# Fused attention and expert routing: 608 slots per expert in place of 640, last tiles of 96 rows, eight result buffers in place of seven

## The chip, the cores and the metric

One core of a Trainium2 chip runs the whole program. The metric is the device time of one execution in microseconds; the runs before are summed up by the median of three. A profiled execution also gives a trace, whose span runs from the first to the last instruction of the core.

## What is computed

A pooled attention feeds a layer of eight experts, each a small two-layer network; every token goes to the one expert that its domain names. Cut to what matters:

```python
# attention: B, H, S, D = 8, 8, 1152, 64; neighbouring queries are averaged in pairs (576 left)
q_pool = q.reshape(B, H, S // 2, 2, D).mean(axis=3)
attn = softmax(q_pool @ k.T / sqrt(D))
x = (attn @ v).transpose(0, 2, 1, 3).reshape(4608, 512)     # one row per token
# experts: w1 is (8, 512, 1024), w2 is (8, 1024, 512)
for e in range(8):
    mask = domain_id == e
    out[mask] = np.maximum(x[mask] @ w1[e], 0.0) @ w2[e]
```

The domains are drawn at random but alike each time. Counted from the drawn input, the experts get 568, 557, 585, 576, 590, 599, 553 and 580 of the 4,608 tokens.

## The kernel before

The program has two stages that overlap. The attention stage computes the tokens' rows batch by batch and writes them in 16-bit form to a table in device memory (x_tok). Vector operations meanwhile work out which token stands in which slot of which expert. Each expert has CAP slots (L48, 640), cut into NTC tiles of 128 (L49): five tiles. Two lists hold, per slot, the row to gather (`grow`) and the row of the output to write (`gid`); a slot that no token fills reads row 0 of x_tok and has an output row beyond the last, whose write is dropped.

The first tiles of the experts 0 to 4 are computed inside the attention stage by `add_tile` (L793), in holes of TensorE's order. What is left is the expert stage from L1049 on, a list of ten *runs* made by `plan_runs` (L926). In this text they are run 0 (three tiles of expert 5, 384 rows), run 1 (one tile, 128 rows), runs 2 to 7 (the last two tiles of an expert each, 256 rows) and runs 8 and 9 (experts 6 and 7 whole, 640 rows). A tile is fetched by `get_x` (L680): an indirect DMA, issued by GpSimd, that gathers 128 rows of x_tok into a buffer `xs`. It must be turned, so that the 512 features lie on the partitions. For runs 2 to 7 TensorE does that (`turn_tile`, L1086, four matmuls against an identity into PSUM, then a copy by VectorE or ScalarE into `xt`); for runs 8 and 9 a transposing DMA on SyncE's queue does it (`flip_x`, L690).

One run is `stage1` (L1065) and `stage2` (L1098). Stage 1 makes the hidden layer: for each of 8 blocks f of 128 hidden units, four matmuls with a block of `w1h` as the weights and the run's slots as the moving columns, in pieces of at most 512 columns; ScalarE (f even) and VectorE (f odd) apply the maximum with 0 and write `hT`. Three PSUM buffers `hp` are shared by this and by the turned tiles. Stage 2 works tile by tile: eight matmuls with a block of `hT` (128 hidden units by the tile's rows) as the weights and 512 columns of `w2h` moving, then a copy of the PSUM result into a buffer `osb2` of the pool `ob` (L1059, seven buffers; ScalarE for a run's last tile and every second one before, VectorE for the others), then an indirect DMA from GpSimd (`scatter`, L525) that writes the tile's rows to the output. The two tiles of the next run are turned between the tiles of stage 2: in a run of two tiles, the first is turned ahead of the first tile's eight matmuls and the second ahead of the second tile's. The last tile of run 9 is split in two halves of 256 columns (L1103 to L1114).

A buffer of `ob` is taken again by the tile seven later, and its copy waits until the scatter that read it has landed. Each engine works its instructions in the order of the program; GpSimd's holds the gathers, the scatters and the weight loads (L509 to L519), whose transfers share one queue, and each of its DMAs waits for the landing of the one eight before it. SyncE's holds the transposing DMAs of runs 8 and 9.

The names in the rows: PE hp L1072 is stage 1, PE op L1117 stage 2, L1108 its split last tile, L1090 a turned tile, L675 a gather, L528 a scatter, L1077 and L1079 the maximum on ScalarE and VectorE, L1123 and L1125 the copies of results, L691 a transposing DMA, L633 the attention's product with v.

Of the kernel before, what the change touches and what calls it, by code (L numbers as in the profile page):

```python
# [9 lines left out]
P = 128  # L10
# [9 lines left out]
def kernel(  # L20
# [10 lines left out]
    nc = tc.nc  # L31
    B, H, S, D = q.shape
    Sp = S // 2
    N, Dm = out.shape
# [10 lines left out]
    NT = B * NQ  # L45
    KO = [0, 128, 256, 384]
    IB = [2 * NQ, 4 * NQ, 6 * NQ]
    CAP = 640  # L48
    NTC = CAP // P  # L49
    W = 432  # L50
    SPP = NC * Sp // W
    DV = D + 2
# [35 lines left out]
    ident16 = perm.tile([P, P], F16, name="ident16")  # L88
# [92 lines left out]
    for i in range(NV):  # L181
# [4 lines left out]
        out=lst[:, :], in_=lst[:, :], compare_op=ALU.is_ge, fill=1.0, base=0,  # L186
# [207 lines left out]
    gid = perm.tile([P, NH], I32, name="gid")  # L394
    grow = perm.tile([P, NH], I32, name="grow")
# [107 lines left out]
    wts = {}  # L503
# [21 lines left out]
    def scatter(dst, src, ap, group, bound=None):  # L525
        nc.gpsimd.memset(gap[:, :], 0.0)
        kw = {} if bound is None else {"bounds_check": bound, "oob_is_err": False}
        ins = nc.gpsimd.indirect_dma_start(  # L528
            out=dst[:, :],
            out_offset=bass.IndirectOffsetOnAxis(ap=ap, axis=0),  # L530
            in_=src,
            in_offset=None,
            **kw,
        )
        tc.declare_no_dep(ins.ins, group=group, reason="rows are unique")
        tc.add_to_no_dep_group(group, ins.ins)
# [136 lines left out]
    def gather(dst, ap, nb=B):  # L673
        nc.gpsimd.memset(gap[:, :], 0.0)
        nc.gpsimd.indirect_dma_start(  # L675
            out=dst, out_offset=None, in_=x_dram[0 : 1 + nb * Sp, :],
            in_offset=bass.IndirectOffsetOnAxis(ap=ap, axis=0),
        )

    def get_x(pool, e, i):  # L680
        x_ = pool.tile([P, Dm], F16, name="xs")
        mark(x_[0:1, 0:1], True)
        nb = [ib // NQ for k_, ib in zip(KO[1:], IB) if (i + 1) * P <= k_] + [B]
        assert len(kept) >= nb[0] * NQ
        gather(x_[:, :], grow[:, e * NTC + i : e * NTC + i + 1], nb[0])
        xs[e, i] = x_

    xs = {}

    def flip_x(dst, e, i):  # L690
        nc.sync.dma_start_transpose(dst, xs[e, i][:, :])  # L691

    WSTEP = [[20 + 40 * e + 10 * j for j in range(4)] for e in range(4)]
    WSTEP.append([174 + 6 * j for j in range(4)])
# [63 lines left out]
    for j in range(NJ):  # L758
        nc.tensor.transpose(
            qt[:, j * QP : (j + 1) * QP], in_=qp[0:QP, j, :, :].rearrange("p h d -> p (h d)"),  # L760
            identity=ident16[0:QP, 0:QP],
# [160 lines left out]
    xt = {0: xf[:, :].rearrange("p (n c) -> p n c", n=ND)}  # L922
    first = [(FILL, i) for i in range(NA)]
# [14 lines left out]
    for p in range(NPAIR - 1):  # L938
        lo = W * (p * SPP + (7 if p < 2 else 3))
# [18 lines left out]
    for t in range(NST + 4):  # L958
# [24 lines left out]
        if t == NST + 1:  # L983
# [3 lines left out]
            e, i0, i1 = next(r for r in runs if (r[0], r[1]) not in xs)  # L987
            for i in range(i0, i1):
                get_x(fxs, e, i)
        if main and want and t >= want[0][2] and t >= last_get + 5 and not (t in later) and not mmq and not rq:  # L990
            e, i, _ = want[0]
# [5 lines left out]
        if first and t >= max(got.get(first[0], NST) + 8, FLIPS[first[0][1]]):  # L997
            e, i = first.pop(0)
# [57 lines left out]
    tb = ctx.enter_context(tc.tile_pool(name="tb", bufs=2, reuse_waits="tile"))  # L1056
    tx = ctx.enter_context(tc.tile_pool(name="tx", bufs=4, reuse_waits="tile"))
    xov = ctx.enter_context(tc.tile_pool(name="xov", bufs=1, reuse_waits="tile"))
    ob = ctx.enter_context(tc.tile_pool(name="ob", bufs=7, reuse_waits="tile"))  # L1059
    wlast.append(ctx.enter_context(tc.tile_pool(name="wnext", bufs=1, reuse_waits="tile")))  # L1060

    def new_xt():
# [2 lines left out]
    def stage1(w1h, xt, m, at=None):  # L1065
        hT = tb.tile([P, NF, CAP], F16, name="hT")
        for f in range(NF):
            hp_ = hps.tile([P, 1024], FP32, name="hp")
            for lo in range(0, m, 512):
                n = min(512, m - lo)  # L1070
                for cc in range(ND):
                    nc.tensor.matmul(  # L1072
                        hp_[:, lo : lo + n], lhsT=w1h[:, cc, f * P : (f + 1) * P],
                        rhs=xt[:, cc, lo : lo + n], start=cc == 0, stop=cc == ND - 1,
                    )
            if f % 2 == 0:
                nc.scalar.activation(hT[:, f, 0:m], hp_[:, 0:m], AF.Relu)  # L1077
            else:
                nc.vector.tensor_scalar(  # L1079
                    out=hT[:, f, 0:m], in0=hp_[:, 0:m], scalar1=0.0, scalar2=None, op0=ALU.max  # L1080
                )
            if at and f in at:
                at[f]()
        return hT

    def turn_tile(dst, x_, i):  # L1086
        ps = hps.tile([P, 1024], FP32, name="hp")
        pv = ps[:, 0 : Dm // 2].bitcast(F16).rearrange("p (c r) -> p c r", c=ND)
        for cc in range(ND):
            nc.tensor.transpose(  # L1090
                pv[:, cc, :], in_=x_[:, cc * P : (cc + 1) * P], identity=ident16[:, :]
            )
        if i % 2 == 0:
            nc.vector.tensor_copy(dst, pv)
        else:
            nc.scalar.copy(dst, pv)

    def stage2(w2h, hT, n, ids, between=(), split=False, first=0):  # L1098
        between = list(between)
        for i in range(n):  # L1100
            for _ in range(-(-len(between) // (n - i)) if i >= first else 0):
                between.pop(0)()
            if split and i == n - 1:  # L1103
                osb = ob.tile([P, Dm], FP32, name="osb2")
                for lo, copy in ((0, nc.vector.tensor_copy), (Dm // 2, nc.scalar.copy)):
                    op_ = ops.tile([P, Dm], FP32, name="op")
                    for f in range(NF):
                        nc.tensor.matmul(  # L1108
                            op_[:, 0 : Dm // 2], lhsT=hT[:, f, i * P : (i + 1) * P],
                            rhs=w2h[:, f, lo : lo + Dm // 2], start=f == 0, stop=f == NF - 1,  # L1110
                        )
                    copy(osb[:, lo : lo + Dm // 2], op_[:, 0 : Dm // 2])
                scatter(out, osb[:, :], ids(i), "oscat", N - 1)
                break  # L1114
            op_ = ops.tile([P, Dm], FP32, name="op")
            for f in range(NF):
                nc.tensor.matmul(  # L1117
                    op_[:, :], lhsT=hT[:, f, i * P : (i + 1) * P], rhs=w2h[:, f, :],
                    start=f == 0, stop=f == NF - 1,
                )  # L1120
            osb = ob.tile([P, Dm], FP32, name="osb2")
            if i % 2 == (n - 1) % 2:
                nc.scalar.copy(osb[:, :], op_[:, :])  # L1123
            else:
                nc.vector.tensor_copy(osb[:, :], op_[:, :])  # L1125
            scatter(out, osb[:, :], ids(i), "oscat", N - 1)

    NR = NPAIR * 2 * NQ

# [37 lines left out]
    for k_, r in enumerate(runs):  # L1167
        e, i0, i1 = r
        n = i1 - i0
        while todo and todo[0][0] <= k_ + 2:  # L1170
            fetch(k_ + 2)
        btw = []
        if k_ == len(runs) - 1:
            nc.gpsimd.drain()
        for kn in (k_ + 1, k_ + 2, k_ + 3):
            if kn >= len(runs) or kn in xt or kn > k_ + 1 and kn < FLIP:
                continue
            xt[kn] = new_xt()
            en, j0, j1 = runs[kn]
            for j in range(j0, j1):  # L1180
                dst = xt[kn][:, :, (j - j0) * P : (j - j0 + 1) * P]
                if kn >= FLIP:
                    flip_x(dst, en, j)
                    continue
                btw.append(lambda dst=dst, en=en, j=j: turn_tile(dst, xs[en, j], j))
        get = lambda: fetch(len(runs))
        part = lambda: wq.pop(0)() if wq else None
        at = {1: get, 4: get, 6: get} if n < NTC else {1: get, 3: get, 5: get}
        if k_ < 2:
            at = {**at, 2: part, 7: part}  # L1190
        elif k_ >= len(runs) - 6:
            at = {**at, 2: part}
        h = stage1(wts[e][0], xt[k_], n * P, at)
        stage2(
            wts[e][1], h, n, lambda i, c=e * NTC + i0: gid[:, c + i : c + i + 1], btw,
            k_ == len(runs) - 1, first=n - 1 if k_ == 0 else 0,
        )
        if k_ in (3, 4):
            check_sums(k_ - 3)
        if i1 == NTC and e == 0 and rest:  # L1200
            er = rest.pop(0)
            fns, wts[er] = load_w(er)
            wq.extend(fns)
# [100 lines left out]
    def one_tile(w, og, oi):  # L1304
        xo = xov.tile([P, Dm], F16, name="xo")
        gather(xo[:, :], og)
        xto = new_xt()
        nc.sync.dma_start_transpose(xto[:, :, 0:P], xo[:, :])
        h = stage1(w[0], xto, P)
        stage2(w[1], h, 1, lambda i: oi)  # L1310

    anyx = nc.values_load(ovi[0:1, E : E + 1], min_val=0, max_val=N + 1)
    with tc.If(anyx > 0):
        bad = nc.values_load(ovi[0:1, E + 1 : E + 2], min_val=0, max_val=1)
        with tc.If(bad > 0):
            again()
            for e in range(E):
                fns, w = load_w(e)
                for fn in fns:
                    fn()  # L1320
                for i in range(NTC):
                    c = e * NTC + i
# [3 lines left out]
        for b in range(B):  # L1326
            for i in range(NQ):
                n = 64 if i == 0 else P
# [4 lines left out]
        for e in range(E):  # L1333
            fns, w = load_w(e)
# [3 lines left out]
            with tc.For_i(0, nt, 1) as j:  # L1338
                oi = xov.tile([P, 1], I32, name="oi")
# [3 lines left out]
                    out=og[:, :], in0=oi[:, :], scalar1=1.0, scalar2=None, op0=ALU.add  # L1343
                )
                nc.vector.tensor_scalar(
                    out=og[:, :], in0=og[:, :], scalar1=float(N), scalar2=None, op0=ALU.min
# [30 lines left out]
```

## Time and profile before

| | us |
|---|---|
| device time, median of 3 runs (lowest to highest) | 417.11 (416.21 to 419.22) |
| device time of the profiled execution | 416.44 |
| its span, first to last instruction | 414.4 |

The device time of the profiled execution lies 2.0 us above its span, and 0.7 us below the median. Stage times below are read from the profiled execution; 0 is the start of its span. "Busy" of TensorE (PE) counts overlapping matmuls once, and the ends of matmuls are modelled, so the time of a group of matmuls is best read from the start of the first to the start of what follows.

### The profile page before, as it was taken

How to read it: one execution, taken by the hardware profiler on the slowest of the kernel's cores; microseconds unless marked ns; L12 is line 12 of the kernel's file. 1: busy time of each engine (PE TensorE's matmuls, PEld its weight loads, DVE VectorE, ACT ScalarE, POOL GpSimd, SP SyncE). 2: the span in 40 equal slices, each digit the busy share in tenths (PEclk: the TensorE clock that was granted, in tenths of full speed). 3: DMA queues.
4: the chain of work that ended last, by engine and by line, in shares of the span. 5: the costliest groups of instructions: out<-in, count | busy, mean ns of one | idle time of the engine just before them, and what ended most of it. 6: DMA issues, size and time to landing. Idle time of an engine off the chain costs nothing.

```text
span 414.4 us, 14867 instructions
## 1 busy us (share of the span) xinstructions
PE 386.7 (93%) x6350; PEld 260.6 (63%) x6350; DVE 232.0 (56%) x638; ACT 331.1 (80%) x396; POOL 182.9 (44%) x303
## 2 busy tenths in 40 slices
PE   8879888888999999999999999999999998999992
PEld 4455555565676776666776676776675766765451
DVE  4488879976565675655756574566534343333231
ACT  5899999999999999999999999999992423323220
POOL 4533222321545554143443344543534875862522
PEclk9899999999999999999999999999999999999998
DMA  8999999995999999989868865969782599999402
GB/s 222 187 220 239 228 238 230 217 228 118 201 212 242 252 224 241 246 193 249 183 152 191 165 152 113 235 152 189 147 161 78 145 137 197 205 154 218 150 25 99
DMA packets 53137, 77.04 MB, mean 186 GB/s; under 512 B 12624, under 2 KB 41841, under 8 KB 53059
## 3 DMA queue, kind: packets, MB, share of 16 engines
q0 software_dynamic: 38336, 66.80, 79.6%
q1 hardware_dynamic: 14450, 9.06, 10.4%
q8 instruction: 51, 0.84, 0.9%
q14 instruction: 28, 0.22, 0.2%
q10 hardware_dynamic: 272, 0.13, 0.1%
HBM read 95.46 MB, written 15.21 MB: 267 GB/s over the span
## 4 chain that ended last, share of the span: by engine, by line
PE 68%; ACT 10%; DMA 8%; DVE 6%; issue 4%; POOL 1%; SPq 1%; POOLq 0%; ACTq 0%; DVEq 0%
PE s L613 17%; PE acc L633 17%; ACT er L621 9%; PE hp L1072 9%; PE op L1117 8%; PE px L821 6%; PE px L808 6%; DMA k<-in_k_dram 4%; DMA out_dram<-osb,gid 3%; PE s L579 3%; DVE kq L584 1%; DMA x_tok<-xb 1%; SPq L664 1%; DVE xb L648 1%; DVE qz L589 1%
## 5 line engine op out<-in xcount | busy, mean ns | idle before, releaser
L621 ACT ACTIVATE er<-s 128x1008 f16<-128x1008 f32 x330 | 299.2, 1096 | 3.7 <-PE s L613 3.1
L633 PE MATMUL acc<-v,er 128*128 128x65 f16 x2835 | 118.3, 194 | 7.3 <-DVE xb L648 3.8
L633 PEld LDWEIGHTS <-er 128*128 128x128 f16 x2880 | 101.0, 98 | 36.7 <-issue 17.6
L613 PE MATMUL s<-qz,kq 64*128 64x504 f16 (+6 forms) x1152 | 113.6, 287 | 7.1 <-ACT er L621 4.2
L675 POOL DMA_INDIRECT xs<-x_tok,grow x40 | 41.2, 1029 | 86.5 <-PE s L613 23.6
L528 POOL DMA_INDIRECT out_dram<-osb,gid x40 | 41.9, 1047 | 69.0 <-DVE osb L827 29.5
L613 PEld LDWEIGHTS <-kq 64*128 64x128 f16 x1152 | 44.7, 94 | 39.6 <-issue 22.3
L116 POOL DMA_DIRECT2D vs<-in_v_dram x32 | 23.7, 741 | 52.8 <-DVE v L554 17.1
L1117 PE MATMUL op<-w2h,hT 128*128 128x512 f16 x200 | 45.8, 379 | 0.0
L1072 PEld LDWEIGHTS <-w1h 128*128 128x128 f16 x384 | 33.7, 98 | 15.6 <-issue 1.8
L1072 PE MATMUL hp<-xt,w1h 128*128 128x256 f16 (+2 forms) x352 | 42.0, 277 | 1.5 <-ACT hT L1077 1.5
L1079 DVE TENSOR_SCALAR hT<-hp 128x256 f16<-128x256 f32 (+3 forms) x40 | 20.1, 504 | 37.0 <-PE hp L1072 29.1
L1123 ACT COPY osb<-op 128x512 f32<-128x512 f32 x14 | 8.2, 586 | 39.9 <-PE op L1117 35.2
L1077 ACT ACTIVATE hT<-hp 128x256 f16<-128x256 f32 (+3 forms) x40 | 17.7, 449 | 23.9 <-PE hp L1072 23.9
L584 DVE COPY kq<-s 128x1152 f16<-128x1152 f16 x31 | 23.4, 756 | 20.3 <-PE s L579 17.6
L1117 PEld LDWEIGHTS <-hT 128*128 128x128 f16 x200 | 19.0, 98 | 20.0
L808 PE MATMUL px<-xt,w1h 128*128 128x128 f16 x448 | 30.8, 219 | 0.0
L821 PE MATMUL px<-w2h,h 128*128 128x512 f16 x112 | 30.6, 381 | 0.0
L544 DVE TENSOR_TENSOR qp<-q 96x768 f16<-96x768 f32 x31 | 29.3, 946 | 2.2 <-DMA q<-in_q_dram 2.1
L646 DVE RECIPROCAL cum<-acc 128x5 f32<-128x5 f32 x47 | 9.0, 192 | 37.8 <-PE acc L633 37.7
L808 PEld LDWEIGHTS <-w1h 128*128 128x128 f16 x448 | 25.3, 98 | 4.9 <-issue 4.7
L813 DVE TENSOR_SCALAR h<-px 128x512 f16<-128x512 f32 x28 | 19.3, 690 | 15.3 <-PE px L808 15.3
(150 smaller groups left out, 347.0 us busy)
## 6 DMA issues: line engine op xcount, KB each, us to landing
q<-in_q_dram POOLq DMA_DIRECT2D x28, 576.0 KB, 9.5
vs<-in_v_dram POOLq DMA_DIRECT2D x32, 288.0 KB, 7.5
k<-in_k_dram POOLq DMA_DIRECT2D x31, 288.0 KB, 6.1
w1h<-in_moe_w_dram POOLq DMA_DIRECT2D x16, 512.0 KB, 11.7
w2h<-in_moe_w_dram POOLq DMA_DIRECT2D x16, 512.0 KB, 8.6
x_tok<-xb SPq DMA_DIRECT2D x23, 96.0 KB, 6.4
q<-in_q_dram SPq DMA_DIRECT2D x3, 576.0 KB, 6.6
x_tok<-xb SPq DMA_DIRECT2D x23, 64.0 KB, 4.8
```

Of the source, the lines that this page charges most:

```text
L116: nc.gpsimd.dma_start(vs[:, :, :, :], v[b, h : h + 2].rearrange("h (p c) d -> p h c d", p=P))
L528: ins = nc.gpsimd.indirect_dma_start(out=dst[:, :], out_offset=bass.IndirectOffsetOnAxis(ap=ap, axis=0), in_=src, in_offset=None, **kw,)
L544: nc.vector.tensor_tensor(out=qp[0:QP, :, :, :].rearrange("p j h d -> p h j d"), in0=q2[:, :, :, 0:D], in1=q2[:, :, :, D : 2 * D], op=ALU.add,
L584: nc.vector.tensor_copy(kq[p][:, :].rearrange("p (c r k) -> p r c k", c=NC, r=2), mt[:, :, 0 : NC * 64].rearrange("p r (c k) -> p r c k", ...
L613: nc.tensor.matmul(s[:, r, o : o + n], lhsT=kq[p][lo:hi, c * P : (c + 1) * P], rhs=qz[p % 2][lo:hi, q0 : q0 + n], start=True, stop=True,)
L621: nc.scalar.activation(er[:, :, o : o + w], st.pop(k)[:, :, 0:w], AF.Exp, bias=0.0, scale=0.0625)
L633: nc.tensor.matmul(acc[p, h][:, i * (D + 1) : (i + 1) * (D + 1)], lhsT=er[:, h, o : o + P], rhs=v16[p % NV][:, c, h, 0 : D + 1], start=c = ...
L675: nc.gpsimd.indirect_dma_start(out=dst, out_offset=None, in_=x_dram[0 : 1 + nb * Sp, :], in_offset=bass.IndirectOffsetOnAxis(ap=ap, axis=0),)
L808: nc.tensor.matmul(m[:, f % 4, :], lhsT=wts[e][0][:, cc, f * P : (f + 1) * P], rhs=h0["xt"][:, cc, :], start=cc == 0, stop=cc == ND - 1,)
L821: nc.tensor.matmul(h0["o"][:, :], lhsT=h0["h"][:, f, :], rhs=wts[e][1][:, f, :], start=f == 0, stop=f == NF - 1,)
L1072: nc.tensor.matmul(hp_[:, lo : lo + n], lhsT=w1h[:, cc, f * P : (f + 1) * P], rhs=xt[:, cc, lo : lo + n], start=cc == 0, stop=cc == ND - 1,)
L1117: nc.tensor.matmul(op_[:, :], lhsT=hT[:, f, i * P : (i + 1) * P], rhs=w2h[:, f, :], start=f == 0, stop=f == NF - 1,)
```

## The change

Slots per expert go from 640 to 608, so the fifth tile of each expert has 96 rows; everything that works on such a tile is cut to its rows; and the pool of result buffers has eight buffers.

```diff
-    CAP = 640
-    NTC = CAP // P
+    CAP = 608
+    NTC = -(-CAP // P)
+    ROWS = [min(P, CAP - i * P) for i in range(NTC)]
...
-        gather(x_[:, :], grow[:, e * NTC + i : e * NTC + i + 1], nb[0])
+        n = ROWS[i]
+        gather(x_[0:n, :], grow[0:n, e * NTC + i : e * NTC + i + 1], nb[0])
...
-        nc.sync.dma_start_transpose(dst, xs[e, i][:, :])
+        nc.sync.dma_start_transpose(dst, xs[e, i][0 : ROWS[i], :])
...
-    ob = ctx.enter_context(tc.tile_pool(name="ob", bufs=7, reuse_waits="tile"))
+    ob = ctx.enter_context(tc.tile_pool(name="ob", bufs=8, reuse_waits="tile"))
...
-                pv[:, cc, :], in_=x_[:, cc * P : (cc + 1) * P], identity=ident16[:, :]
+                pv[:, cc, 0:n], in_=x_[0:n, cc * P : (cc + 1) * P], identity=ident16[0:n, 0:n]
...
-                    op_[:, :], lhsT=hT[:, f, i * P : (i + 1) * P], rhs=w2h[:, f, :],
+                    op_[0:r, :], lhsT=hT[:, f, i * P : i * P + r], rhs=w2h[:, f, :],
...
-                nc.scalar.copy(osb[:, :], op_[:, :])
+                nc.scalar.copy(osb[0:r, :], op_[0:r, :])
...
-            scatter(out, osb[:, :], ids(i), "oscat", N - 1)
+            scatter(out, osb[0:r, :], ids(i), "oscat", N - 1)
...
-        h = stage1(wts[e][0], xt[k_], n * P, at)
+        rows = ROWS[i0:i1]
+        h = stage1(wts[e][0], xt[k_], sum(rows), at)
```

The largest expert has 599 tokens, so 608 slots hold all of them. No instruction is added, removed or moved on any engine. Their sizes change: runs 2 to 7 have 224 columns in stage 1 in place of 256, and runs 8 and 9 have 512 and 96 in place of 512 and 128. The waits of the result copies change too. ScalarE's order in runs 2 to 4 reads as follows before (the osb copies are numbered 7826 for run 2, 7932 for run 3, 8029 for run 4; DMASW6 and the like are the eight counters of GpSimd's DMAs):

```order
L1123 COPY osb_7826<-op 128x512 [waits PE_49]
L1077 ACTIVATE hT<-hp 128x256 [waits DVE_49,PE_49,Activation_49]
L1077 ACTIVATE hT<-hp 128x256 [waits PE_49] x3
L1096 COPY xt<-hp 128x4x128 [waits PE_49]
L1123 COPY osb_7932<-op 128x512 [waits DMASW6_49,PE_49]
L1077 ACTIVATE hT<-hp 128x256 [waits DVE_49,PE_49,Activation_49]
L1077 ACTIVATE hT<-hp 128x256 [waits PE_49] x3
L1096 COPY xt<-hp 128x4x128 [waits PE_49]
L1123 COPY osb_8029<-op 128x512 [waits DMASW0_49,PE_49]
```

and with the change:

```order
L1127 COPY osb_7826<-op 96x512 [waits PE_49]
L1079 ACTIVATE hT<-hp 128x224 [waits DVE_49,PE_49,Activation_49]
L1079 ACTIVATE hT<-hp 128x224 [waits PE_49] x3
L1099 COPY xt<-hp 128x4x128 [waits PE_49]
L1127 COPY osb_7932<-op 96x512 [waits PE_49]
L1079 ACTIVATE hT<-hp 128x224 [waits DVE_49,PE_49,Activation_49]
L1079 ACTIVATE hT<-hp 128x224 [waits PE_49] x3
L1099 COPY xt<-hp 128x4x128 [waits PE_49]
L1127 COPY osb_8029<-op 96x512 [waits DMASW7_49,PE_49]
```

Run 3's last copy, the eighth result, has lost its wait for a scatter; the later ones wait for the scatter of one tile earlier than before. On TensorE, the place in run 4 where the second tile of run 5 is turned reads before:

```order
L1117 LDWEIGHTS hT [waits Activation_49]
L1117 MATMUL op<-w2h,hT 128x512
L1117 LDWEIGHTS hT [waits DVE_49]
L1117 MATMUL op<-w2h,hT 128x512
L1090 LDWEIGHTS xs [waits DMASW1_49]
L1090 MATMUL hp<-ident_104,xs 128x128
```

and with the change:

```order
L1121 LDWEIGHTS hT [waits Activation_49]
L1121 MATMUL op<-w2h,hT 128x512
L1121 LDWEIGHTS hT [waits DVE_49]
L1121 MATMUL op<-w2h,hT 128x512
L1093 LDWEIGHTS xs [waits DMASW1_49]
L1093 MATMUL hp<-ident_104,xs 128x96
```

The wait for the gather of that tile stands there in both; the matmuls that turn it have 96 columns.

## Rows read from the trace of the kernel before

**Rows 1.** The page, parts 1, 2 and 5.

```profile
PE 386.7 (93%) x6350; PEld 260.6 (63%) x6350; DVE 232.0 (56%) x638; ACT 331.1 (80%) x396; POOL 182.9 (44%) x303
PE   8879888888999999999999999999999998999992
PEclk9899999999999999999999999999999999999998
...
L633 PE MATMUL acc<-v,er 128*128 128x65 f16 x2835 | 118.3, 194 | 7.3 <-DVE xb L648 3.8
```

**Rows 2.** Busy time by stretch, expert stage; first row names the columns.

```profile
core 0: us, PE busy (x) PEld busy (x) DVE busy (x) ACT busy (x) POOL busy (x), PEclk, DMA share, GB/s
...
330.00:340.00 10.00, 10.00 (x77) 6.68 (x76) 3.36 (x11) 3.58 (x8) 8.56 (x15) 1.00 1.11 162
340.00:350.00 10.00, 8.69 (x63) 5.66 (x62) 4.46 (x11) 2.50 (x6) 4.46 (x10) 1.00 1.10 170
...
405.00:414.40 9.40, 2.17 (x18) 1.54 (x16) 1.12 (x2) 0.37 (x1) 2.68 (x5) 0.86 0.26 89
```

**Rows 3.** Groups by line and shape, 320 to 415 us: busy us, mean ns, idle before.

```profile
L1117 PE MATMUL op<-w2h,hT 128*128 128x512 f16 x187 | 43.0, 379 | 0.0
L1072 PEld LDWEIGHTS <-w1h 128*128 128x128 f16 x352 | 30.7, 98 | 13.5 <-issue 1.8
...
L1072 PE MATMUL hp<-xt,w1h 128*128 128x256 f16 x192 | 22.1, 273 | 1.3 <-ACT hT L1077 1.3
...
L1072 PE MATMUL hp<-xt,w1h 128*128 128x512 f16 x64 | 16.4, 379 | 0.0
...
L1072 PE MATMUL hp<-xt,w1h 128*128 128x128 f16 x96 | 8.4, 219 | 0.2 <-ACT hT L1077 0.2
...
L1108 PE MATMUL op<-w2h,hT 128*128 128x256 f16 x16 | 2.0, 272 | 0.0
```

**Rows 4.** Timeline of runs 3 and 4: start us, length us, instruction, [idle before].

```profile
334.14 3.66 PE L1072 MATMUL hp<-xt,w1h 128*128 128x256 f16 x32
...
334.98 1.00 POOL L675 DMA_INDIRECT xs<-x_tok,grow  x1 [0.23 <-issue]
...
341.54 1.47 PE L1072 MATMUL hp<-xt,w1h 128*128 128x256 f16 x12
...
343.40 0.59 ACT L1123 COPY osb<-op 128x512 f32<-128x512 f32 x1 [4.75 <-DMA out_dram<-osb,gid]
...
344.32 2.34 PE L1072 MATMUL hp<-xt,w1h 128*128 128x256 f16 x20 [1.31 <-ACT hT L1077]
...
346.49 0.98 POOL L675 DMA_INDIRECT xs<-x_tok,grow  x1 [1.24 <-DMA out_dram<-osb,gid]
346.50 0.39 PE L1090 MATMUL hp<-ident,xs 128*128 128x128 f16 x4
...
348.23 0.42 PEld L1090 LDWEIGHTS <-xs 128*128 128x128 f16 x4
348.45 0.39 PE L1090 MATMUL hp<-ident,xs 128*128 128x128 f16 x4
```

**Rows 5.** Waits, 320 to 415 us: who, for whom, us in total, times, longest.

```profile
ACT osb L1123 <- DMA out_dram<-osb,gid: 4.7, 1, 4.7
```

**Rows 6.** The chain that ended last, in order of time: start us, us.

```profile
205.42 1.16 PE acc L633 x35
...
331.05 12.27 DMA out_dram<-osb,gid
...
365.48 3.49 PE hp L1072 x32
...
372.43 8.69 PE hp L1072 x64
381.12 8.63 PE op L1117 x40
```

**Rows 7.** DMAs issued 337.1 to 338.0 us: count, median us to landing.

```profile
xs<-x_tok,grow POOLq DMA_INDIRECT x1, 12.8
```

**Rows 8.** SyncE's queue, 300 to 415 us: its timeline, then its waits.

```profile
330.48 42.30 SPq L691 DMA_TRANSPOSE xt<-xs  x10
...
SPq L1313 <- SPq L1313: 11.8, 3, 6.0
```

More of the change, by code (lines that the diff above doesn't have):

```diff
@@ L1086, in turn_tile @@
     def turn_tile(dst, x_, i):
+        n = ROWS[i]
         ps = hps.tile([P, 1024], FP32, name="hp")
@@ L1090, in turn_tile, with stage2 @@
             nc.tensor.transpose(
-                pv[:, cc, :], in_=x_[:, cc * P : (cc + 1) * P], identity=ident16[:, :]
+                pv[:, cc, 0:n], in_=x_[0:n, cc * P : (cc + 1) * P], identity=ident16[0:n, 0:n]
             )
         if i % 2 == 0:
-            nc.vector.tensor_copy(dst, pv)
+            nc.vector.tensor_copy(dst, pv[:, :, 0:n])
         else:
-            nc.scalar.copy(dst, pv)
-    def stage2(w2h, hT, n, ids, between=(), split=False, first=0):
+            nc.scalar.copy(dst, pv[:, :, 0:n])
+    def stage2(w2h, hT, rows, ids, between=(), split=False, first=0):
         between = list(between)
-        for i in range(n):
+        n = len(rows)
+        for i, r in enumerate(rows):
             for _ in range(-(-len(between) // (n - i)) if i >= first else 0):
@@ L1108, in stage2 @@
                         nc.tensor.matmul(
-                            op_[:, 0 : Dm // 2], lhsT=hT[:, f, i * P : (i + 1) * P],
+                            op_[0:r, 0 : Dm // 2], lhsT=hT[:, f, i * P : i * P + r],
                             rhs=w2h[:, f, lo : lo + Dm // 2], start=f == 0, stop=f == NF - 1,
                         )
-                    copy(osb[:, lo : lo + Dm // 2], op_[:, 0 : Dm // 2])
-                scatter(out, osb[:, :], ids(i), "oscat", N - 1)
+                    copy(osb[0:r, lo : lo + Dm // 2], op_[0:r, 0 : Dm // 2])
+                scatter(out, osb[0:r, :], ids(i), "oscat", N - 1)
                 break
@@ L1122, in stage2 @@
             if i % 2 == (n - 1) % 2:
-                nc.scalar.copy(osb[:, :], op_[:, :])
+                nc.scalar.copy(osb[0:r, :], op_[0:r, :])
             else:
-                nc.vector.tensor_copy(osb[:, :], op_[:, :])
-            scatter(out, osb[:, :], ids(i), "oscat", N - 1)
+                nc.vector.tensor_copy(osb[0:r, :], op_[0:r, :])
+            scatter(out, osb[0:r, :], ids(i), "oscat", N - 1)
     NR = NPAIR * 2 * NQ
@@ L1180 @@
             for j in range(j0, j1):
-                dst = xt[kn][:, :, (j - j0) * P : (j - j0 + 1) * P]
+                dst = xt[kn][:, :, (j - j0) * P : (j - j0) * P + ROWS[j]]
                 if kn >= FLIP:
@@ L1192 @@
             at = {**at, 2: part}
-        h = stage1(wts[e][0], xt[k_], n * P, at)
+        rows = ROWS[i0:i1]
+        h = stage1(wts[e][0], xt[k_], sum(rows), at)
         stage2(
-            wts[e][1], h, n, lambda i, c=e * NTC + i0: gid[:, c + i : c + i + 1], btw,
+            wts[e][1], h, rows, lambda i, c=e * NTC + i0: gid[0 : rows[i], c + i : c + i + 1], btw,
             k_ == len(runs) - 1, first=n - 1 if k_ == 0 else 0,
@@ L1309, in one_tile @@
         h = stage1(w[0], xto, P)
-        stage2(w[1], h, 1, lambda i: oi)
+        stage2(w[1], h, [P], lambda i: oi)
     anyx = nc.values_load(ovi[0:1, E : E + 1], min_val=0, max_val=N + 1)
```

## The prediction, made before the changed kernel ran

> **What bounds the kernel now.** I read the page first. TensorE is busy 93% of the span and at full granted clock from end to end, but for the first and last slices [rows 1]. Since the change touches only the expert stage, I then read that stage in stretches of ten microseconds. [...]
>
> The timeline names the stall. Run 4's stage 1 starts at 341.54 and stops after 12 matmuls: all three PSUM buffers are full, ScalarE has not yet emptied the first. ScalarE stands at the copy of run 3's last result until 343.40, 4.75 us, for a scatter [rows 4]. It is the only wait of this kind in the stage [rows 5]. The chain shows which scatter: the first of run 0, issued at 331.05 and landed 12.27 us later [rows 6]. It is the eighth result that waits for the first result's buffer.
>
> **The change part by part.**
>
> *Narrower stage 1.* Durations of matmuls in the table are latencies (273 ns for 256 columns), so I take start to start from the chain: 32 matmuls of 256 columns in 3.49 us are 109 ns each, 64 of a whole expert (32 of 512, 32 of 128) in 8.69 us, and 40 of stage 2 with 512 columns in 8.63 us, 216 ns each [rows 6]. Then the 128-column ones take (8.69 - 32 x 0.216)/32 = 0.056 us. All three are columns / 2.4 GHz plus 2.4 to 2.7 ns, so 32 columns fewer are worth 13.3 ns: 256 becomes 96 ns, 128 becomes 42 ns. Is there a floor? Each matmul here has its own weight load of 98 ns [rows 3], but the attention's 65-column matmuls, with the same loads, follow each other every 33 ns (35 in 1.16 us) [rows 1, 6]; 42 lies above that, so I count the full 13.3. The counts are 192 of 256 columns and 64 of the 128-column ones (the other 32 of 96 are run 1, unchanged) [rows 3]: 256 x 13.3 ns = 3.41 us, 0.427 a run. Bounds: 3.41 if linear; about 1.7 if a pair could not go below the load's 98 ns plus 2.4 (192 x 8.7 ns, nothing for the rest). I take linear, since 55 and 33 ns pairs stand in the rows.
>
> *Narrower turned tiles.* Six last tiles, four matmuls each, 13.3 ns: 0.32 us. All of it is on PE's path.
>
> *ScalarE and VectorE* have shorter maxima, hidden under PE. They matter at a run's start, where ScalarE first copies a result (0.59 us) and PE needs its third buffer back: PE now arrives at its fourth block after 1.15 us in place of 1.31. Copy and maximum end some 1.05 us after the run's start, so I count nothing; if the cover goes, at most 0.05 to 0.1 us a run.
>
> *Stage 2* keeps its 216 ns: its columns are w2's 512, and only the weights shrink to 96 columns. Row first: a load of 128 columns takes 98 ns and lies under the 216 ns of the matmul before it [rows 3, 6]. The trace has no load of 96 columns, so I bound it from 0 (hidden, as every load here) to 98 ns each (fully in the open); I take 0. [...]
>
> *The eighth buffer.* Run 3's last copy no longer waits, so the 1.31 us stall goes. Later copies wait for a scatter one tile earlier than now; none of them waits now, so none will. What is late next? PE turns run 5's second tile in run 4, at 348.45, from the gather that GpSimd issued at 334.98, and did not wait for it: its weight load began at 348.23 [rows 4]. Without the stall and with 3 x 0.427 + 3 x 0.053 us saved by then, PE would be there at 348.45 - 1.31 - 1.28 - 0.16 = 345.70. When does the gather land? The scatters ahead of it in the same queue held GpSimd until just before 346.49 [rows 4]; the queue's neighbours took 12.27 and 12.8 us to land [rows 6, 7], which gives 347.3 to 347.8. I take 347.1, between 346.4 and 347.8. So a new wait stands at this place. Some of it goes: this gather and one before it have 96 rows, and SyncE's first transposing DMAs, which share the transfer engines and start when run 2 frees its buffer (330.48) [rows 8], start 0.4 us earlier. I take 0.5 off: landed at 346.6, PE on at 346.8. That is 1.65 saved at this point in place of 2.75. Ends: the gather unchanged at 347.8 (0.45 saved here), or landed in time (2.75).
>
> *After that* each step stays: this tile's own turn 0.05, stage 1 of runs 5 to 7 1.28, two more turned tiles 0.11, runs 8 and 9 0.85: 2.29. Run 9 needs its turned tiles at about 389.6; SyncE had seen the last of them landed by 372.8 + 11.8 = 384.6 [rows 8], and the last is needed only after four 512-column matmuls, 390.5. Four microseconds earlier, 1.9 us are left.
>
> *The end.* The last tile's copies and scatter follow PE as now; the scatter has 96 rows of 128, worth 0 to 0.25 us; I take 0.1.
>
> Sum: 1.65 + 2.29 + 0.1 = 4.0 us, with ends at 2.8 and 5.4. The profiled execution took 416.44 us, so 412.4; set against the median, which is 0.7 us higher, 417.11 - 4.0 = 413.1.
>
> **The rivals.** *The gather is in time.* If the queue drains faster or GpSimd's 96-row gathers are issued quicker, nothing replaces the stall: 2.75 + 2.29 + 0.1 = 5.1, 412.0. For it: the landing lies only about a microsecond behind PE. Against it: the DMA share is above 1 just there [rows 2].
>
> *Narrow matmuls have a floor.* With 8.7 ns saved per 256-column matmul and nothing on the rest, PE arrives later at the gather, waits less, and after it saves only 3 x 0.28 + 0.1: 1.65 + 0.95 + 0.1 = 2.7, 414.4. Against it speak the 33 ns pairs.
>
> *Run 9's tiles come late.* The transposing DMAs do not depend on PE; if they slip 4 us (two of the ten now have 96 rows, and the queue is shared), 2 us of the gain turn into a wait: 415.1. For it: the slack is 1.9 us. Against it: fewer bytes move.
>
> *Slower: the 96-column loads stand in the open.* Seven last tiles have 8 loads each and the split tile 16: 72 loads in stage 2. At 98 ns each that is 7.1 us, more than the 4.0 gained: 420.2. It decides from 56 ns a load. For it: no row has a load this narrow. Against it: all loads in the expert stage, 128 columns each, hide.
>
> **How the numbers follow.** The forecast, 413.1, has 0.58; the gather in time 0.20; the floor 0.08; run 9's tiles late 0.08; the open loads 0.06. One per cent, about what a measurement of this kernel can tell from no change, is 4.17 us, so the border is at 412.9, right beside the forecast. Of the forecast I put four tenths below it, of the gather in time nine tenths: 0.23 + 0.18, 0.41 faster. Slower by over 1% (421.3) needs the open loads and more: 0.03. The rest, 0.56, is within 1%. The range goes from 411.6, the gather in time with half a microsecond of noise, to 415.6, run 9's tiles late with as much; it leaves out the open loads and the edges.
>
> **What would show it.** Right: stage 1 of runs 2 to 7 takes 3.07 us each and of runs 8 and 9 8.26; no ScalarE wait at the eighth result; PE idle 0.5 to 1.5 us ahead of the second turned tile of run 4, released by the gather; stage 2 still 1.73 us a tile. Wrong: 32 matmuls of 224 columns take 3.2 us or more (floor); stage 2's last tiles take longer than the others (open loads); PE waits at the start of run 9 (turned tiles); or another copy waits for a scatter.

## The result, and the profile after

| | us |
|---|---|
| kernel before, median of 6 runs beside the changed one (lowest to highest) | 416.66 (415.44 to 419.22) |
| changed kernel, median of 6 runs | 412.46 (410.94 to 414.18) |
| ratio, with its 95% interval | 0.9898 (0.9863 to 0.9932) |
| profiled execution after: device time, span | 410.94, 408.8 |

The change saves 4.2 us, 1.0%, at the very border that the prediction set between faster and within 1%. (Ratios leave disturbed runs out, so they need not be the quotient of the medians.) Run 0 starts at 310.82 in the profiled execution, at 311.53 before; ahead of it no instruction has changed, so these 0.7 us are the execution's. The stage from there to the end is what the change can touch. Its row for the kernel before, with the columns of [rows 2]:

```profile
311.53:414.40 102.87, 94.15 (x658) 57.61 (x654) 33.80 (x87) 29.23 (x61) 55.08 (x99) 0.99 0.73 142
```

and for the changed kernel, with the stretches that answer to [rows 2]:

```profile
310.82:408.80 97.98, 90.47 (x657) 57.58 (x653) 32.36 (x87) 28.41 (x61) 54.41 (x99) 0.97 0.73 145
...
330.00:340.00 10.00, 10.00 (x77) 6.93 (x76) 4.36 (x14) 2.54 (x7) 8.54 (x15) 1.00 1.10 237
340.00:350.00 10.00, 10.00 (x89) 8.09 (x87) 4.67 (x15) 4.25 (x11) 8.15 (x17) 1.00 0.94 224
399.44:408.80 9.36, 2.04 (x17) 1.66 (x15) 1.11 (x2) 0.37 (x1) 2.42 (x5) 0.73 0.24 81
```

The stage is 4.9 us shorter. TensorE (PE) bounds it in both traces: busy 94.15 of 102.87 us before and 90.47 of 97.98 after, at granted clocks of 0.99 and 0.97. Its busy time falls by 3.68, and PE has no hole left between 330 and 350, where 1.31 us stood. The DMAs moved 237 GB/s from 330 to 340, against 162 before. The end gained nothing: 9.36 us from the split tile's first matmul on, 9.2 before.

The chain, as [rows 6], shows the widths:

```profile
339.96 3.07 PE hp L1074 x32
...
344.98 0.17 PE hp L1093 x4
...
347.02 1.15 PE hp L1074 x12
...
348.17 2.08 PE hp L1074 x20
...
367.54 8.27 PE hp L1074 x64
375.80 8.63 PE op L1121 x40
...
399.61 0.89 PE op L1112 x8
```

32 matmuls of 224 columns take 3.07 us in place of 3.49, a whole expert's stage 1 8.27 in place of 8.69; stage 2 keeps its 8.63. Run 5 alone, at 347.02, takes 3.23: PE stops for 0.16 us after its 12th matmul, until ScalarE's first maximum has emptied a PSUM buffer. That maximum starts late, released by VectorE's part (L1152) of a sum that the kernel makes just ahead of run 5 and that uses a PSUM buffer too:

```profile
347.76 0.80 ACT L1079 ACTIVATE hT<-hp 128x224 f16<-128x224 f32 x2 [0.26 <-DVE tot L1152]
```

Before, the same maximum followed ScalarE's copy at once and run 5 took 3.49 like the others. Busy time doesn't show a stop as short as this, since a matmul of 224 columns counts as busy for 259 ns and the next starts after 96. The timeline of runs 3 and 4, as [rows 4]:

```profile
332.88 3.23 PE L1074 MATMUL hp<-xt,w1h 128*128 128x224 f16 x32
...
333.94 0.96 POOL L676 DMA_INDIRECT xs<-x_tok,grow  x1 [0.23 <-issue]
...
339.80 3.23 PE L1074 MATMUL hp<-xt,w1h 128*128 128x224 f16 x32
340.00 0.58 ACT L1127 COPY osb<-op 96x512 f32<-96x512 f32 x1 [3.04 <-PE op L1121]
...
342.87 0.39 PE L1093 MATMUL hp<-ident,xs 128*128 128x128 f16 x4
...
344.82 0.34 PE L1093 MATMUL hp<-ident,xs 96*128 96x96 f16 x4
```

Run 3's last copy, at 340.00, waits for its matmuls only. The second turned tile of run 4, at 344.82, has no idle time ahead of it: the wait that was forecast there is not there. Its gather, issued at 333.94, has its last completion in the trace at 339.6; before it was 346.9. The first scatter was issued at 330.01 and complete at 337.1, 7.1 us later, not 12.27. So by this execution's landing seven buffers would have done as well, and the question is whether the change made the queue faster or the execution did.

Groups by line and shape, as [rows 3]:

```profile
L1121 PE MATMUL op<-w2h,hT 128*128 128x512 f16 x144 | 32.9, 379 | 0.0
L1074 PE MATMUL hp<-xt,w1h 128*128 128x224 f16 x192 | 19.5, 259 | 0.0
L1121 PEld LDWEIGHTS <-hT 128*128 128x128 f16 x144 | 13.7, 98 | 14.5
L1121 PE MATMUL op<-w2h,hT 128*96 128x512 f16 x56 | 13.2, 379 | 0.0
L1121 PEld LDWEIGHTS <-hT 128*96 128x96 f16 x56 | 6.5, 123 | 4.3
L1112 PEld LDWEIGHTS <-hT 128*96 128x96 f16 x16 | 1.8, 123 | 0.3
L1093 PEld LDWEIGHTS <-xs 96*128 96x128 f16 x24 | 1.7, 97 | 1.2
```

A weight load of 96 columns takes longer than one of 128, 123 ns against 98, and stays hidden.

### The profile page after: what moved, and what is told of

Read it like the earlier page. It is cut to its first block, busy times and chain, and to the rows that moved or that the text cites. A ratio compares the mean times of both kernels' runs of the same rounds, so it can differ in the third digit from the quotient of the medians.

```text
span 408.8 us, 14866 instructions
## 1 busy us (share of the span) xinstructions
PE 381.4 (93%) x6350; PEld 259.7 (64%) x6350; DVE 230.3 (56%) x638; ACT 330.1 (81%) x396; POOL 182.0 (45%) x303
## 4 chain that ended last, share of the span: by engine, by line
PE 73%; ACT 9%; DVE 7%; DMA 5%; issue 3%; SPq 1%; POOL 0%; POOLq 0%; ACTq 0%; DVEq 0%
PE s L614 18%; PE acc L634 17%; PE op L1121 11%; PE hp L1074 10%; ACT er L622 8%; PE px L823 6%; PE px L810 6%; DMA k<-in_k_dram 3%; PE s L580 3%; DVE kq L585 1%; SPq L665 1%; DVE xb L649 1%; DMA x_tok<-xb 1%; DVE dal L222 1%; DVE qz L590 1%
## 5 line engine op out<-in xcount | busy, mean ns | idle before, releaser
L1121 PE MATMUL op<-w2h,hT 128*128 128x512 f16 (+1 forms) x200 | 45.8, 379 | 0.0
L1074 PEld LDWEIGHTS <-w1h 128*128 128x128 f16 x384 | 32.6, 98 | 12.1 <-issue 0.5
L1074 PE MATMUL hp<-xt,w1h 128*128 128x224 f16 (+3 forms) x352 | 38.6, 267 | 0.2 <-ACT hT L1079 0.2
L1127 ACT COPY osb<-op 128x512 f32<-128x512 f32 (+1 forms) x14 | 8.2, 583 | 37.8 <-PE op L1121 37.8
L1081 DVE TENSOR_SCALAR hT<-hp 128x224 f16<-128x224 f32 (+3 forms) x40 | 19.1, 478 | 33.2 <-PE hp L1074 26.9
L1079 ACT ACTIVATE hT<-hp 128x224 f16<-128x224 f32 (+3 forms) x40 | 17.0, 427 | 21.9 <-PE hp L1074 21.5
L1121 PEld LDWEIGHTS <-hT 128*128 128x128 f16 (+1 forms) x200 | 20.2, 105 | 18.8
L810 PEld LDWEIGHTS <-w1h 128*128 128x128 f16 x448 | 25.3, 98 | 4.9 <-issue 4.7
```

The source lines that it names most:

```text
L810: nc.tensor.matmul(m[:, f % 4, :], lhsT=wts[e][0][:, cc, f * P : (f + 1) * P], rhs=h0["xt"][:, cc, :], start=cc == 0, stop=cc == ND - 1,)
L1074: nc.tensor.matmul(hp_[:, lo : lo + n], lhsT=w1h[:, cc, f * P : (f + 1) * P], rhs=xt[:, cc, lo : lo + n], start=cc == 0, stop=cc == ND - 1,)
L1121: nc.tensor.matmul(op_[0:r, :], lhsT=hT[:, f, i * P : i * P + r], rhs=w2h[:, f, :], start=f == 0, stop=f == NF - 1,)
```

## The experiments

Three theories of the stall. A: the queue is as slow as in the first trace of before, and the eighth buffer took the stall away. B: the transfers of 96 rows drain the queue faster. C: the queue's speed differs from execution to execution, and the buffer helps only where the queue is slow. Three sets of four kernels ran, each beside runs of the kernel before.

### First set, on a chip where all is slower

Seven buffers with 608 slots:

```diff
-    ob = ctx.enter_context(tc.tile_pool(name="ob", bufs=8, reuse_waits="tile"))
+    ob = ctx.enter_context(tc.tile_pool(name="ob", bufs=7, reuse_waits="tile"))
```

> 608 slots with seven result buffers. Three theories. A, the eighth buffer took the stall away: the first scatter of run 0 lands some 12 us after its issue as before (12.27 us), run 3's last copy waits for it again, and as the narrower stage 1 brings TensorE there about 1 us earlier, the stall is 1.3 to 2.3 us; the time is 1.3 to 2.3 us above that of the changed kernel, 413.8 to 414.8. B, the 96-row gathers and scatters drain the queue faster (7.1 us for that scatter in the changed kernel's trace): no ScalarE wait for a scatter, no stall, 412.5. C, how fast the queue drains differs from execution to execution whatever the rows: a mean stall below 1.3 us, 412.5 to 413.5, and a trace that may show either.

Eight with 640 slots. The 32 columns less in `xt`, `hT` and `xf` are what makes room for the eighth buffer (4 x 256 + 2 x 512 + 256 bytes of a partition, against 2,048). With 640 slots that room is missing, so results 8, 16 and 24 go to `xf`, the buffer of run 0's turned tiles:

```diff
...
+        if made[0] % 8 == 0 and made[0] <= 25:
+            return xf[:, 0 : 2 * Dm].bitcast(FP32)
...
```

> 640 slots with an eighth result buffer (results 8, 16 and 24 are written to the buffer that held run 0's turned tiles, which is free by then, since a pool of eight does not fit beside 640 slots). A: the stall of 1.31 us at run 4 goes and nothing takes its place before 347.1, the time falls by 1.3 us to 415.4; stage 1 keeps 3.49 us a run. B: the same, and the first scatter still takes about 12 us, as its rows are 128. C: the time falls by the mean of a stall that is not always there, 0 to 1.3 us, and the landing of that scatter is anywhere between 7 and 12 us after its issue.

Both kernels once more, unchanged:

> The kernel before once more, for a second trace. A and B: the first scatter of run 0 lands about 12 us after its issue, ScalarE waits 4 to 5 us for it at run 3's last copy, and TensorE stalls 1.3 us in run 4. C: landing, wait and stall differ, down to none.

> The changed kernel once more, for a second trace. B: the first scatter lands about 7 us after its issue, the gather of run 5's second tile by 340, and nothing waits. A and C: the drain may be slow this time (12 us), then the gather lands near 346.6 and TensorE waits 0.5 to 1.5 us ahead of run 4's second turned tile, as the prediction had it. The prediction's own forecast for the columns holds in any case: 32 matmuls of 224 columns in 3.07 us.

Measured: before 438.81 (median of 23), 608 with seven 437.76, ratio 0.9994 (0.9952 to 1.0037), 640 with eight 439.28, 1.0004 (0.9961 to 1.0046); of the unchanged two, one execution each, 438.32 and 439.19. None can be told from before, which is 22 us slower than in the first pair. The stage rows, of before

```profile
321.45:436.20 114.75, 98.67 (x658) 58.99 (x654) 34.08 (x87) 29.12 (x61) 55.09 (x99) 0.96 0.63 127
```

and of the changed kernel:

```profile
322.76:437.20 114.44, 95.80 (x658) 59.58 (x654) 32.36 (x87) 28.42 (x61) 54.48 (x99) 0.93 0.56 125
...
366.00:368.00 2.00, 1.98 (x11) 1.62 (x12) 1.09 (x4) 0.36 (x1) 1.78 (x3) 0.50 0.23 88
```

PE's work shrinks here too, by 2.9 us, but its holes grow from 16.1 to 18.6 (stage less busy time), and the stage is 0.3 shorter. In the first pair the holes were 8.7 and 7.5, most of that time behind the last matmul. One hole of the changed kernel, in its timeline:

```profile
366.02 1.30 PE L1074 MATMUL hp<-xt,w1h 128*128 128x224 f16 x6 [6.69 <-DVE xt L1097]
```

Behind a hole of 6.69 us the granted clock is 0.50. With holes like these the narrower matmuls bought nothing that can be measured here. Where PE has no hole, this trace has the times of the first pair: run 7's stage 1 takes 3.07 us, runs 8 and 9 have 8.27, and run 5 again 3.23.

The times don't tell the theories apart, but the second trace of before does say something. Not all DMA completions are in the traces of this chip, so the landing of run 0's first scatter can't be read. GpSimd, however, holds each DMA back until the one eight before it has landed. In the first trace of before, the DMA eight behind that scatter was issued at 344.14, 0.8 us after the landing at 343.32 and after 3.86 us of idle time. In the second trace of before the two are

```profile
341.14 1.05 POOL L528 DMA_INDIRECT out_dram<-osb,gid  x1 [0.24 <-issue]
...
350.62 1.03 POOL L528 DMA_INDIRECT out_dram<-osb,gid  x1 [0.26 <-issue]
```

with no more idle time than any DMA has. So the scatter landed within 9.5 us, and the 12 us that A and B expected did not come back. The same two instructions lie 9.4 or 9.5 us apart, without a wait, in all eight traces of the two slower chips, with 128 rows and with fewer.

### Second set, on a chip as fast as in the first pair

> The changed kernel once more, timed against the kernel before. The first pair of kernels ran on one chip (416.7 and 412.5); on a second chip the kernel before took 438.8 and one look at the changed kernel 439.2. Theory 1, the gain is one of TensorE's and is the same 4 to 5 us wherever TensorE bounds the expert stage: ratio 0.988 to 0.992 if the kernel before is back near 417. Theory 2, on a chip where the expert stage is held by its transfers and not by TensorE (109 us and more for the stage in place of 103), narrower matmuls buy nothing: ratio 0.997 to 1.003 if the kernel before is near 439.

> 608 slots with seven result buffers, as before in the first set of runs but beside the changed kernel. A, the eighth buffer took the stall away: 1.3 to 2.3 us above the changed kernel, and the trace has ScalarE waiting for a scatter at run 3's last copy. B, the narrower transfers drain the queue faster: no such wait, and within 0.5 us of the changed kernel. C, the drain differs from execution to execution: the mean lies 0 to 1.3 us above.

> 640 slots with eight result buffers, beside the kernel before. A and B: 1.3 us below the kernel before if that one stalls as in its first trace; C: 0 to 1.3 us below. Together with the run of 608 slots and seven buffers this splits the gain: if the two parts add up, this gain plus that of 608 slots alone is that of the change.

The fourth kernel takes the gathers alone back to 128 rows:

```diff
-        n = ROWS[i]
-        gather(x_[0:n, :], grow[0:n, e * NTC + i : e * NTC + i + 1], nb[0])
+        gather(x_[:, :], grow[:, e * NTC + i : e * NTC + i + 1], nb[0])
```

> The change, but the gathers of the last tiles fetch 128 rows again (everything behind them uses 96). B, if the narrower gathers are what drains the queue faster: the first scatter of run 0 lands some 12 us after its issue again, the gather of run 5's second tile lands near 346, TensorE waits 0.5 to 1.5 us for it, and the time is about 1.1 us above the changed kernel. Else: within 0.5 us of the changed kernel, with the same landings as there (7 us).

The times are medians of 9 to 12 runs, that of before of 32:

| kernel | us | ratio to before, interval | stage in its trace |
|---|---|---|---|
| before | 415.88 | | |
| 640 slots, eight buffers | 415.62 | 0.9982 (0.9952 to 1.0012) | 101.51 |
| 608 slots, seven buffers | 412.62 | 0.9910 (0.9879 to 0.9942) | 97.93 |
| 608 slots, eight buffers (the change) | 412.36 | 0.9905 (0.9873 to 0.9937) | 97.91 |
| the change, gathers of 128 rows | 412.72 | 0.9907 (0.9873 to 0.9940) | 97.60 |

The gain is back, inside the 0.988 to 0.992 that the first theory of the changed kernel's expectation gave. Slots and buffers add up: by the medians 608 slots bring 3.26 us with either count of buffers, and the buffer 0.26 with either count of slots. By the ratios it is 3.2 and 3.7 us for the slots, 0.2 and 0.75 for the buffer. Each ratio is uncertain by about 1.3 us, so the buffer's part can't be told from nothing, and the slots' part can. The stage row of 640 slots with eight buffers, a stage without a stall, has PE busy as before:

```profile
313.79:415.30 101.51, 94.03 (x658) 57.61 (x653) 33.84 (x87) 29.29 (x61) 54.97 (x99) 0.98 0.69 144
```

against 608 slots with seven:

```profile
311.07:409.00 97.93, 90.57 (x658) 57.58 (x654) 32.49 (x87) 28.30 (x61) 54.46 (x99) 0.99 0.72 146
```

PE has 3.46 us less work and the stage is 3.58 shorter, with neither stall nor eighth buffer in the sum: that is the columns alone. Seven buffers do make ScalarE wait in this trace:

```profile
340.50 0.58 ACT L1127 COPY osb<-op 96x512 f32<-96x512 f32 x1 [3.25 <-DMA out_dram<-osb,gid]
...
368.64 0.58 ACT L1127 COPY osb<-op 96x512 f32<-96x512 f32 x1 [4.16 <-DMA out_dram<-osb,gid]
```

and in PE's timeline, run 4's stage 1 and what follows it:

```profile
340.08 3.38 PE L1074 MATMUL hp<-xt,w1h 128*128 128x224 f16 x32
343.30 0.39 PE L1093 MATMUL hp<-ident,xs 128*128 128x128 f16 x4
```

The eighth copy starts 0.2 us later than its matmuls allowed, since run 0's first scatter, issued at 330.47, was complete only then; the other wait lies at the start of run 8. The first cost PE 0.15 us: from start to start run 4 takes 3.22 us in place of 3.07. The second cost nothing, since run 8's stage 1 has its 8.27. Read the release, not the length of the wait: of the 3.25 us, 3.04 pass in every run until PE is done.

From issue to the last of its completions that scatter took 7.1 us in the first trace of the changed kernel and 10.1 in the second, of the same program. With seven buffers it took 9.9, with 640 slots and eight 8.7, with gathers of 128 rows 10.5, in the first trace of before 12.3. So A falls: 12.3 is the worst of six, and the kernel before itself landed within 9.5 us on two other chips. B falls as the explanation: with gathers of 128 rows the scatter took 10.5 us, with 96 rows 7.1, 9.9 and 10.1, and the times overlap; a small effect of the rows is not excluded by so few traces. C is what is left. It is not shown in its strict form, as no program is known to have been traced twice on one chip: what differs may be the execution or the chip. The eighth copy is ready 9.2 to 10.7 us after that issue, so that seven buffers make it, or would make it, 0.2 to 1.7 us late in four of these six executions. PE forgives little of it: a copy 1.7 us late cost 1.47 in the first trace of before (run 4's stage 1 from start to start, 4.96 for 3.49 us), one 0.2 us late cost 0.15 here.

The gather of run 5's second tile, the one that was forecast to be late, came in time in all six traces of the faster chips, though narrowly in two. In the second trace of the change it is complete at 344.8 and PE is there at 345.0:

```profile
345.18 0.34 PE L1093 MATMUL hp<-ident,xs 96*128 96x96 f16 x4
```

With gathers of 128 rows it was complete at 345.3, 0.8 us ahead of PE.

### Third set, on another slower chip

> The change, with the last tile of each expert cut to its tokens rounded up to 16 (64, 48, 80, 64, 80, 96, 48 and 80 rows in place of 96); left out is that an expert with more tokens than these rows would be noticed. 208 columns fewer in all. If a matmul of stage 1 costs its columns / 2.4 GHz plus a constant all the way down: 208 x 32 / 2.4 GHz = 2.77 us in stage 1 and 144 x 4 / 2.4 GHz = 0.24 us in the turned tiles, 3.0 us below the changed kernel, some 409.4; a run with 176 columns takes 32 x 13.3 ns x 1.5 = 0.64 us less than one with 224, 2.43 us. If a pair of load and matmul cannot go below the load's 98 ns plus 2.4, the 224-column matmuls, at 96 ns, are there already, and the gain is 0 to 0.5 us. If narrower weights (48 to 80 columns) make loads that stand in the open, stage 2's last tiles take more than 1.73 us.

```diff
+    LASTS = [64, 48, 80, 64, 80, 96, 48, 80]
+    ROWS = [[P] * (NTC - 1) + [n] for n in LASTS]
```

Six buffers (the edit of the first kernel with 6):

> 608 slots with six result buffers: run 3's first copy (VectorE) waits for the first scatter of run 0, its last for the second. In the traces so far that scatter lands 7.1 to 12.3 us after its issue, and the seventh copy comes some 8 us after the issue. C: a wait of 0 to 4 us, by these landings 1.8 on average; TensorE forgives some 0.4 us of it, as in the first trace (copy 1.7 us late, stall 1.3), so 0.5 to 2.5 us above the changed kernel, about 1.5. If scatters were not what the copies wait for, no change.

> The kernel before once more, for another trace. C: the first scatter lands 7 to 12 us after its issue; the eighth copy is ready 10.7 us after it, so that only a landing above that makes ScalarE wait, and most likely neither ScalarE nor TensorE waits this time. A and B: 12 us, ScalarE waits 4 to 5 us and TensorE stalls 1.3 us.

```diff
-        for kn in (k_ + 1, k_ + 2, k_ + 3):
+        for kn in (k_ + 1, k_ + 2):
```

> The change, with the transposing DMAs of run 8's tiles issued one run later, into another buffer, so that they start after about 335 in place of 329 to 331. If these DMAs are what slows GpSimd's queue, the first scatter lands at most 8 us after its issue, as it does with no transposing packets beside it, and the time stays within 0.5 us of the changed kernel, since nothing waits there. If they are not, it lands 7 to 12 us after its issue as in the other traces. If run 8's tiles then come late, TensorE waits at the start of run 8 (367 to 372) and the time rises.

Measured: before 436.32 (median of 29); rows by expert 436.48, ratio 1.0028 (0.9993 to 1.0063); six buffers 436.71, 1.0013 (0.9971 to 1.0055); transposing DMAs later 438.01, 1.0024 (0.9989 to 1.0059); before, one more execution, 442.67. Nothing changes the time on this chip, the 3.0 us expected of rows by expert included, and again not all completions are there. So six buffers and the later transposing DMAs are inconclusive: where PE's holes lie elsewhere, neither can show, and what sets the speed of GpSimd's queue stays open. In the two traces of the first pair, the scatters that had no packets of the other data queue, q1, beside them landed 2.7 to 7.4 us after their issue, in the eight cases where the landing can be read. Rows by expert still answer how narrow matmuls behave, in a stretch where PE runs at a granted clock of 1.00 with hardly a hole. The timeline of that kernel:

```profile
367.92 3.15 PE L1075 MATMUL hp<-xt,w1h 128*128 128x192 f16 x32
370.90 0.39 PE L1093 MATMUL hp<-ident,xs 128*128 128x128 f16 x4
...
378.16 0.38 PE L1093 MATMUL hp<-ident,xs 128*128 128x128 f16 x4 [0.20 <-DVE hT L1082]
...
388.53 7.87 PE L1075 MATMUL hp<-xt,w1h 128*128 128x512 f16 x64
396.24 8.90 PE L1121 MATMUL op<-w2h,hT 128*128 128x512 f16 x40
405.08 8.23 PE L1075 MATMUL hp<-xt,w1h 128*128 128x512 f16 x64
413.14 7.07 PE L1121 MATMUL op<-w2h,hT 128*128 128x512 f16 x32
```

From start to start, 32 matmuls of 512 and 32 of 48 columns take 7.71 us, with 80 columns 8.06. By the prediction's rule (0.417 ns a column, the slope from 3.49 / 32 us for 256 columns to 8.63 / 40 us for 512, plus 2.5 ns, with 216 ns for 512) they are 7.63 and 8.06: no floor at the load's 98 ns, down to 48 columns. The run of 192 columns, run 5 again, takes 2.98 us where the rule gives 2.64. Its matmuls follow each other every 82 ns, as the rule has it, but for three stops, after 8, 12 and 16 of them, 0.35 us together; each ends within 0.1 us of VectorE or ScalarE emptying a PSUM buffer. The run behind it ends in a stop of the same kind, 0.20 us of idle time for VectorE's maximum. So the rival of a floor is refuted for the matmuls; what slows narrow runs in its place is the pace of the maxima, seen here (0.35 and 0.20 us) and in run 5 of the change (0.16 us).

## Why the prediction was right, step by step

The forecast was 413.1, a saving of 4.0 us; measured were 412.46 and 4.2 beside the first set of before, 412.36 and 3.5 beside the second. The columns were right and, by the second set, make up nearly all of the gain. That the whole came so close is luck in part: the stall's two terms, 1.31 us gained and 1.10 lost again, were both wrong and nearly cancel.

- *Stage 1* was right: 3.07 us a run and 8.27 a whole expert, as forecast to 0.01, 8 x 0.42 = 3.36 us for 3.41. Its rate, 2.4 columns a nanosecond, is the slope of the measured times of before: 8.63 / 40 less 3.49 / 32 us for 256 columns, 0.417 ns a column. Run 5 is the exception, with 3.23 us.
- *Turned tiles* were right: 0.22 to 0.17 us, six times 0.05 for the forecast 0.32. Together with stage 1: 3.68 us of PE's busy time, forecast 3.73; less run 5's stop, which busy time doesn't show, 3.5.
- *ScalarE and VectorE*: "I count nothing; if the cover goes, at most 0.05 to 0.1 us a run". The cover went in one run of six, run 5, and cost 0.16 us there in each of the three traces of 608 slots with eight buffers on the faster chips.
- *Stage 2* was right: 8.63 for 40 and 1.73 for 8. The loads became slower (98 to 123 ns, 1.26 times) and stayed hidden, also in the split tile: 0.89 us for eight matmuls of 256 columns, before and after. So the rival of loads in the open falls. A load of 96 columns takes longer than the 98 ns that the prediction set as the most it could cost, and costs nothing, as it is hidden.
- *The eighth buffer* is the step that failed, in both of its terms. "So a new wait stands at this place": it did not, in any of the four traces of 608 slots on the faster chips. "I take 0.5 off: landed at 346.6" should have been a spread: it landed 28.8 to 33.6 us after run 0's start, not 35.1, with PE there at 33.8. And "so the 1.31 us stall goes" booked as a fixed gain what the second set puts at 0.2 to 0.75 us on average. Both errors come from one reading, a single execution's landing times taken for the kernel's. Two smaller ones: the stall's idle time is 1.31 us, but start to start it cost 1.47; and of ScalarE's 4.75 us "for a scatter", 3.09 pass in every run until PE is done.
- *The end* was wrong by its 0.1 us: nothing gained. The ends of the sum, 2.8 and 5.4, come out as 2.7 and 5.3 from its own terms (0.45 + 2.29 and 2.75 + 2.29 + 0.25).
- *The rival* that the gather is in time is what happened in the profiled pair: 3.5 for the columns + 1.47 for the stall - 0.15 for the longer end = 4.82 of the 4.89 measured, forecast 5.1. Its time of 412.0 is as near to the medians as the forecast's, but with its stall term the mean gain would be too large. Run 9's tiles were not late: PE goes from run 8 into run 9 without a hole in the chain.

## What to carry to other kernels

Where PE was the bound here, columns taken from its matmuls came back at 0.417 ns a column, to 0.01 us a run, wherever the engines that empty its PSUM buffers kept up. Narrower runs leave these engines less time (3.07 us for eight maxima in place of 3.49), and the stop of run 5, 0.16 us, is the first sign. A stall for a DMA that one trace shows is a draw from a spread (7 to 12 us for the same scatter here): price it by how often the landing passes the time that the buffers allow, not by its length in that trace. An extra buffer is insurance and worth its mean (0.2 to 0.75 us here), and none of it was seen on a chip where PE waits for other things.

## What the runs showed of the hardware that was not expected

- Loads of fewer columns took longer. In the kernel with rows by expert, on the third chip:

```profile
L1112 PEld LDWEIGHTS <-hT 128*80 128x80 f16 x16 | 1.8, 117 | 0.3
...
L1121 PEld LDWEIGHTS <-hT 128*64 128x64 f16 x16 | 1.6, 109 | 1.4
```

  64, 80 and 96 columns take 109, 117 and 123 ns, 128 columns 98. Fewer rows cost nothing: 96 rows of 128 columns take 97. A load of 123 ns hides even under matmuls that follow each other every 111 ns (0.89 us for eight).
- The kernel before took 416 us on the chip of the second set and 436 to 439 on two others, where its traces have run 0 starting 10 and 13 us later than the first one (321.45 and 324.54) and PE's holes in the stage nearly doubled (16.1 and 16.7 us for 8.7). The 3.3 us that 608 slots bring on the first showed on neither of the others, in any kernel with 608 slots or fewer that was timed there. What makes PE wait on those is not settled: their traces put much of it to "issue" or to releases that they can't name.
- The DMAs differ in speed between executions of one program (and perhaps between chips): between 330 and 340 they moved 237 and 208 GB/s in two traces of the change, with the first scatter at 7.1 and 10.1 us. In the first trace of before it was 162 GB/s and 12.3 us.
